# A spectral-gate and gMLP kernel on one core: the TensorE order written by hand, with second-branch matmuls placed into the transform's waits

## The chip, the cores and the metric

The kernel runs on one core of one Trainium2 chip. The metric is the device time of one execution in microseconds (us). Profiles show the core's span, from its first to its last instruction, which is 1.7 to 2.0 us shorter than the time of the same run. PE is the matrix engine (TensorE), PEld its weight load, DVE is VectorE, ACT is ScalarE, POOL is GpSimd, SP the sync engine, whose queue issues most of the DMAs. PE's results go to PSUM buffers, from which ACT or DVE copies them to SBUF, the on-chip memory: that copy is called the eviction. rstd is one over the square root of variance plus epsilon, bn_stats the DVE instruction that gathers mean and variance (BATCH_NORM_STATS2 in the views), and a slab is a block of 512 rows of `w_sp`, loaded transposed in four pieces.

## The reference

```python
# x, B_x: (1, 2048, 576) bf16     w_in: (576, 4608)     w_sp: (2048, 2048)     w_out: (2304, 576)
xn = layernorm(A_x)
s  = irfft2(rfft2(xn) * (w_r + 1j * w_i))            # branch A: a 2-D Fourier filter
z  = gelu(xn @ w_in)                                 # branch B: gMLP
z1, z2 = z[..., :2304], layernorm(z[..., 2304:])
g  = w_sp @ z2 + b_sp[:, None]
y  = (z1 * g) @ w_out
out = A_x + s * silu(y)
```

(In the reference, branch B is called with the normalised `xn`.)

## The kernel before

Branch A is a chain of matrix products against Fourier tables, and between its stages the data changes layout by going through DRAM:

- `p0`: row block of `xn` times the table of the short axis, evicted and written to DRAM `Ad`.
- `p1`: first half of the long axis; reads `Ad` with another stride, writes `Bd`.
- `p2` and `p3`: second half, multiplied with the filter by DVE in between, and the inverse; reads `Bd`, writes `Ed`.
- `p4`: reads `Ed`, leaves `V` in SBUF. `p5`: `V` to the result `Yd`.

Each of the three passes through DRAM is a wait: the last block must be evicted, written, and read again before the next stage starts. Branch B has much independent work: `z2` (96 units of five 384-column matmuls and one gelu; statistics by DVE on even row blocks, by ACT on odd ones), and then the main loop of 72 steps, each a `z1` tile (5 matmuls) and a `main` tile (16 matmuls), with the output product after each 18 steps.

As program text (cuts are marked):

```python
def ln1(ms):                      # statistics, then normalise, transpose on PE, evict to xnT
    ...
    nc.scalar.activation(out=rs[:], in_=mv[:, :, 1], func=ACT.Sqrt, bias=eps[:], scale=1.0)
    nc.vector.reciprocal(out=rs[:], in_=rs[:])
    for i, m in enumerate(ms):
        ...                       # normalise (DVE), 5 transposes (PE), evict (ACT)

def p0(m):
    ...                           # 10 matmuls
    sg = STG[m % 3]...            # three staging slots
    nc.scalar.activation(out=sg, in_=pa[:, :, 0:L], func=ACT.Identity)
    nc.sync.dma_start(out=Adw[m], in_=sg)

def p23(ch):
    for i in range(0, 8, 2):
        pa = psa.tile(...)        # psa: two buffers, used by p0..p5 and the output
        ...                       # p2: 2 matmuls
        for c in range(2):
            nc.vector.tensor_tensor(out=tt[:, c, :, :], in0=pa..., in1=wt..., op=ALU.mult)
        pb = psa.tile(...)
        ...                       # p3: 4 matmuls on tt, ACT evicts, Ed is written every second pair

with tc.manual_schedule(engines={SP}):       # only the sync queue is in program order
    for ms in ([0], [1], [2, 3], [4, 5, 6, 7], [8, 9, 10, 11], [12, 13, 14, 15]):
        ln1(ms)
        for m in ms: p0(m)
    ...                           # p1_read, load_w, p1, p23_read, p23
    ...                           # constants G4, bias, CESO, first z1 weights
    load_slab(0)                  # four DMA transposes of w_sp
    p4_read(0); p4_read(1)
    for ch in range(4): p4(ch); ...
    for m in range(MT): z2(m)     # 96 units
    z1(0)
    for k in range(NK):
        if q == 0 and 2 * fi < MT: p5(2 * fi); p5(2 * fi + 1)
        ...
        if k + 1 < NK: z1(k + 1)
        main(k)
        ...
```

All engines but SP are ordered by the framework's scheduler at build time. It already moves `z2` matmuls forward into waits of branch A. Once built, the order of a queue is fixed: in experiment 5 PE stands 14.3 us in front of late operands with `z2` work behind them.

Of the kernel before, what the change touches and what calls it, by code (L numbers as in the profile page):

```python
# [11 lines left out]
ACT = mybir.ActivationFunctionType  # L12
# [68 lines left out]
def kernel(  # L81
# [114 lines left out]
    for c in range(1, 4):  # L196
        XC.append(load_x(c))
# [15 lines left out]
    def ln1(ms):  # L213
# [7 lines left out]
        rs = small.tile([P, n], F32, tag=f"rs{n}", bufs=3)  # L221
        nc.scalar.activation(out=rs[:], in_=mv[:, :, 1], func=ACT.Sqrt, bias=eps[:], scale=1.0)
        nc.vector.reciprocal(out=rs[:], in_=rs[:])
        for i, m in enumerate(ms):
            xn = XN[m % 3]
            nc.vector.tensor_scalar(out=xn[:, 0:D], in0=XC[m // 4][:, m % 4, :], scalar1=mv[:, i, 0:1],  # L226
                                    scalar2=rs[:, i:i + 1], op0=ALU.subtract, op1=ALU.mult)
            pt = psh.tile([P, KS, P], BF16, tag="h")
            for ks in range(KS):
                nc.tensor.transpose(pt[:, ks, :], xn[:, ks * P:(ks + 1) * P], ident[:])  # L230
            nc.scalar.activation(out=xnT[:, m, :, :], in_=pt[:], func=ACT.Identity)
# [3 lines left out]
    def p0(m):  # L235
# [5 lines left out]
        sg = STG[m % 3].rearrange("p (c l) -> p c l", c=2)  # L241
        nc.scalar.activation(out=sg, in_=pa[:, :, 0:L], func=ACT.Identity)
        nc.sync.dma_start(out=Adw[m], in_=sg)
# [7 lines left out]
    def p1(ch):  # L251
        ain = AIN[ch]
        av = ain.rearrange("p (s l) -> p s l", s=8)
        bs = BES[ch % 2]
        bv = bs.rearrange("p (s l) -> p s l", s=8)
        for i in range(0, 8, 2):
            pa = psa.tile([P, 2, 512], F32, tag="a")
            for j in range(2):
                nc.tensor.matmul(pa[:, j, 0:L], lhsT=G1[:, ch * 8 + i + j, :], rhs=av[:, i + j, :], start=True, stop=True)
            nc.scalar.activation(out=bv[:, i:i + 2, :], in_=pa[:, :, 0:L], func=ACT.Identity)  # L260
        nc.sync.dma_start(out=rowv(Bd)[:, ch * 8 * L:(ch + 1) * 8 * L], in_=bs)
# [8 lines left out]
    def p23_read(ch):  # L270
        nc.sync.dma_start(out=AIN[ch].rearrange("p (h l) -> p h l", h=8), in_=colv(Bd)[:, ch * 8:(ch + 1) * 8, :])

    def p23(ch):
        ain = AIN[ch].rearrange("p (h l) -> p h l", h=8)
        for i in range(0, 8, 2):
            hh = ch * 8 + i
            wt = WCH[(hh // 4) % 2]
            tt = TT[(i // 2) % 2]
            pa = psa.tile([P, 2, 512], F32, tag="a")
            for j in range(2):  # L280
                nc.tensor.matmul(pa[:, j, 0:L], lhsT=MM[:, 0, :], rhs=ain[:, i + j, :], start=True, stop=True)  # L281
            for c in range(2):
                nc.vector.tensor_tensor(out=tt[:, c, :, :], in0=pa[:, :, 0:L], in1=wt[:, c, hh % 4:hh % 4 + 2, :], op=ALU.mult)  # L283
            pb = psa.tile([P, 2, 512], F32, tag="a")
            for j in range(2):
                for c in range(2):
                    nc.tensor.matmul(pb[:, j, 0:L], lhsT=MM[:, 1 + c, :], rhs=tt[:, c, j, :], start=(c == 0), stop=(c == 1))  # L287
            es = BES[ch % 2].rearrange("p (h l) -> p h l", h=8)
            nc.scalar.activation(out=es[:, i:i + 2, :], in_=pb[:, :, 0:L], func=ACT.Identity)
            if i % 4 == 2:  # L290
                if hh // 4 + 2 < 8:
                    load_w(hh // 4 + 2)
                nc.sync.dma_start(out=colv(Ed)[:, hh - 2:hh + 2, :], in_=es[:, i - 2:i + 2, :])
# [208 lines left out]
```

## Time and profile before

| what | value | view |
|---|---|---|
| time, median of 4 runs | 580.79 us (579.43 to 582.55) | times |
| span of the profiled run (a fifth run, of 578.61 us) | 576.8 us | page |
| sum of all matmuls at their issue pace | about 533 us | order of time, summed |
| first `z1` (start of the main loop) | 161.4 us | order of time, PE |
| PE idle by name before that | 26 us | waits, PE |

The page's first part gives engine, busy time, share of the span and instructions. In its second part one digit stands for 1/40 of the span (14.4 us), in tenths; PEclk is the TensorE clock that was granted.

```profile
PE 545.3 (95%) x3128; PEld 301.3 (52%) x3128; DVE 208.6 (36%) x413; ACT 172.5 (30%) x342; POOL 21.8 (4%) x77
...
PE   4798988999699999999999999999999999999996
...
PEclk9898999999799999999999999999999999999999
```

PE is the only engine that is busy throughout. But for the tail, all that is missing lies in the first 11 digits, 160 us. From the groups of instructions by line (busy, mean ns of one, idle before and its releaser) this is the largest matmul group:

```profile
L388 PE MATMUL pg<-AR,z 128*128 128x512 bf16 x1152 | 260.6, 379 | 0.0
```

379 ns is how long one takes, not how often one starts: matmuls overlap. In the order of time, the first of 16 of L388 starts 3.45 us before the group that follows, so one starts every 216 ns. The sum of such paces is the floor, about 533 us, to which 7 us of start and 5 us of tail are added.

The waits of PE (engine, line, for whom: us in total, times, longest):

```profile
PE pt L230 <- DVE AR L226: 12.0, 4, 6.9
PE pa L304 <- DMA AR<-Ed: 4.3, 1, 4.3
PE pb L287 <- DVE AR L283: 4.2, 5, 1.2
PE pa L259 <- DMA AR<-Ad: 2.1, 1, 2.1
PE ph L341 <- ACT z L347: 2.0, 2, 1.2
```

They are spread: the start, the `Ad` read, the multiplies in p2/p3 (L283), the `Ed` read. The largest single DMA wait has its origin in the sync queue. In order of time (start, us, engine, line, operation, count), the sync queue issues:

```profile
131.96 13.77 SPq L370 DMA_TRANSPOSE AR<-in_B_w_sp_dram  x4
145.77 1.06 SPq L296 DMA_DIRECT2D AR<-Ed  x2
```

Four transposes of the slab take 13.77 us to issue, and the `Ed` read stands behind them. This is one pass through p2/p3 on PE, with the idle time before a group in brackets:

```profile
87.28 0.41 PE L281 MATMUL pa<-AR 128*128 128x289 bf16 x2
87.53 1.30 PE L341 MATMUL ph<-RW,xnT 128*128 128x384 bf16 x7
90.03 0.30 PE L287 MATMUL pb<-AR 128*128 128x289 bf16 x1 [1.20 <-DVE AR L283]
```

`p2` (L281), then the `z2` matmuls that the scheduler put into the wait, then `p3` (L287), still 1.2 us too early for the multiplies.

### The profile page before, as it was taken

How to read it: one execution, taken by the hardware profiler on the slowest of the kernel's cores; microseconds unless marked ns; L12 is line 12 of the kernel's file. 1: busy time of each engine (PE TensorE's matmuls, PEld its weight loads, DVE VectorE, ACT ScalarE, POOL GpSimd, SP SyncE). 2: the span in 40 equal slices, each digit the busy share in tenths (PEclk: the TensorE clock that was granted, in tenths of full speed). 3: DMA queues.
4: the chain of work that ended last, by engine and by line, in shares of the span. 5: the costliest groups of instructions: out<-in, count | busy, mean ns of one | idle time of the engine just before them, and what ended most of it. 6: DMA issues, size and time to landing. Idle time of an engine off the chain costs nothing.

```text
span 576.8 us, 7798 instructions
## 1 busy us (share of the span) xinstructions
PE 545.3 (95%) x3128; PEld 301.3 (52%) x3128; DVE 208.6 (36%) x413; ACT 172.5 (30%) x342; POOL 21.8 (4%) x77
## 2 busy tenths in 40 slices
PE   4798988999699999999999999999999999999996
PEld 2575545555455544447544444754444474444464
DVE  6602367864563432223322222332222232222223
ACT  3856976778461211110111111111111111111101
POOL 2000111112010000000000000000000000000000
PEclk9898999999799999999999999999999999999999
DMA  8737485549613249311661111164111122111003
GB/s 300 214 94 248 160 228 164 161 116 254 174 58 92 73 121 251 95 51 32 136 143 32 31 32 51 55 149 108 32 31 32 51 63 73 31 32 53 0 12 92
DMA packets 80965, 59.47 MB, mean 103 GB/s; under 512 B 36768, under 2 KB 75552, under 8 KB 80672
## 3 DMA queue, kind: packets, MB, share of 16 engines
q1 hardware_dynamic: 80928, 58.97, 37.3%
q8 instruction: 24, 0.39, 0.3%
q14 instruction: 13, 0.11, 0.1%
HBM read 38.74 MB, written 11.82 MB: 88 GB/s over the span
## 4 chain that ended last, share of the span: by engine, by line
PE 81%; ACT 5%; DVE 4%; SPq 4%; DMA 3%; issue 2%; POOL 1%; DVEq 0%; ACTq 0%; POOLq 0%
PE pg L388 43%; PE ph L380 13%; PE po L402 12%; PE ph L341 5%; SPq L370 2%; PE pa L239 2%; PE pa L319 2%; ACT TH L350 2%; DMA AR<-in_A_x_dram 1%; DVE st L348 1%; DVE AR L283 1%; PE pa L304 1%; PE pb L287 1%; DMA AR<-Ed 1%; DMA AR<-Ad 1%
## 5 line engine op out<-in xcount | busy, mean ns | idle before, releaser
L388 PE MATMUL pg<-AR,z 128*128 128x512 bf16 x1152 | 260.6, 379 | 0.0
L388 PEld LDWEIGHTS <-z 128*128 128x128 bf16 x1152 | 112.7, 98 | 135.6
L391 DVE TENSOR_TENSOR AR<-pg,AR 128x512 bf16<-128x512 f32 x72 | 49.8, 691 | 230.4 <-PE pg L388 230.4
L382 ACT ACTIVATE AR<-ph 128x512 bf16<-128x512 f32 x72 | 42.9, 597 | 241.7 <-PE ph L380 241.7
L341 PE MATMUL ph<-RW,xnT 128*128 128x384 bf16 x480 | 90.2, 333 | 2.0 <-ACT z L347 2.0
L380 PE MATMUL ph<-xnT,AR 128*128 128x512 bf16 x360 | 89.5, 379 | 0.0
L402 PE MATMUL po<-AR,RW 128*128 128x288 bf16 x576 | 71.2, 286 | 0.0
L341 PEld LDWEIGHTS <-xnT 128*128 128x128 bf16 x480 | 47.7, 100 | 32.4 <-issue 6.4
L402 PEld LDWEIGHTS <-RW 128*128 128x128 bf16 x576 | 56.4, 98 | 14.9
L380 PEld LDWEIGHTS <-AR 128*128 128x128 bf16 x360 | 35.1, 98 | 40.2
L348 DVE BATCH_NORM_STATS2 st<-z 128x6 f32<-128x384 bf16 x48 | 24.1, 548 | 31.4 <-ACT z L347 31.4
L406 ACT ACTIVATE TH<-po 128x576 f32<-128x576 f32 x16 | 10.4, 651 | 77.6 <-PE po L402 77.6
L392 DVE TENSOR_TENSOR RW<-AR 128x512 bf16<-128x512 bf16 x72 | 30.6, 425 | 6.7
L407 DVE SCALAR_TENSOR_TENSOR AR<-TH,po 128x576 bf16<-128x576 f32 x16 | 12.1, 754 | 47.5 <-ACT TH L406 47.5
L345 ACT ACTIVATE z<-ph 128x384 bf16<-128x384 f32 x48 | 23.6, 493 | 10.9 <-PE ph L341 10.6
L283 DVE TENSOR_TENSOR AR<-pa,AR 128x578 bf16<-128x578 f32 x32 | 22.7, 751 | 5.1 <-PE pa L281 5.0
L347 ACT ACTIVATE z<-ph 128x384 bf16<-128x384 f32 x48 | 21.1, 495 | 5.8 <-PE ph L341 5.7
L239 PE MATMUL pa<-AR,xnT 128*128 128x289 bf16 x160 | 22.4, 299 | 0.2
L239 PEld LDWEIGHTS <-xnT 128*128 128x128 bf16 x160 | 16.1, 102 | 5.8 <-issue 0.3
L362 DVE TENSOR_SCALAR z<-z,mv,rs 128x2304 bf16<-128x2304 bf16 x16 | 14.1, 879 | 13.9 <-POOL rs L210 13.9
L230 PE MATMUL pt<-ident,AR 128*128 128x128 bf16 x80 | 7.1, 248 | 12.0 <-DVE AR L226 12.0
L287 PE MATMUL pb<-AR 128*128 128x289 bf16 x64 | 12.9, 288 | 5.0 <-DVE AR L283 4.2
(50 smaller groups left out, 241.0 us busy)
## 6 DMA issues: line engine op xcount, KB each, us to landing
AR<-in_B_w_in_dram SPq DMA_DIRECT2D x24, 384.0 KB, 3.5
AR<-in_A_x_dram SPq DMA_DIRECT2D x20, 144.0 KB, 2.3
AR<-in_B_w_out_dram SPq DMA_DIRECT2D x1, 2592.0 KB, 12.3
Ad<-AR SPq DMA_DIRECT2D x16, 144.5 KB, 2.6
AR<-Ad SPq DMA_DIRECT2D x4, 578.0 KB, 5.6
AR<-in_A_w_r_dram SPq DMA_DIRECT2D x16, 144.5 KB, 2.9
AR<-in_A_w_i_dram SPq DMA_DIRECT2D x16, 144.5 KB, 3.3
Bd<-AR SPq DMA_DIRECT2D x4, 578.0 KB, 3.3
```

The source lines that it names most:

```text
L239: nc.tensor.matmul(pa[:, c, 0:L], lhsT=xnT[:, m, ks, :], rhs=CDSD[:, ks, c, :], start=(ks == 0), stop=(ks == KS - 1))
L283: nc.vector.tensor_tensor(out=tt[:, c, :, :], in0=pa[:, :, 0:L], in1=wt[:, c, hh % 4:hh % 4 + 2, :], op=ALU.mult)
L341: nc.tensor.matmul(ph[:], lhsT=xnT[:, m, ks, :], rhs=WIN2[:, ks, n * ZC:(n + 1) * ZC], start=(ks == 0), stop=(ks == KS - 1))
L345: nc.scalar.activation(out=zc, in_=ph[:], func=ACT.Gelu_apprx_tanh, accum_out=sm[:, n:n + 1])
L347: nc.scalar.activation(out=zc, in_=ph[:], func=ACT.Gelu_apprx_tanh)
L348: nc.vector.bn_stats(out=st[:, n, :], in_=zc)
L380: nc.tensor.matmul(ph[:].rearrange("p (a t) -> p a t", a=4), lhsT=wb[:, ks, (fi % WG) * P:(fi % WG + 1) * P], rhs=xnT[:, 4 * q:4 * q + 4, ...
L382: nc.scalar.activation(out=Z1T[k % 3], in_=ph[:], func=ACT.Gelu_apprx_tanh)
L388: nc.tensor.matmul(pg[:], lhsT=Z2[m][:, fi * P:(fi + 1) * P], rhs=SLAB[q % 2][:, m, :], start=(m == 0), stop=(m == MT - 1))
L391: nc.vector.tensor_tensor(out=tmp, in0=pg[:], in1=BB[:, q * 512:(q + 1) * 512], op=ALU.add)
L392: nc.vector.tensor_tensor(out=U[k % NU], in0=tmp, in1=Z1T[k % 3], op=ALU.mult)
L402: nc.tensor.matmul(po[:, h, 0:H2], lhsT=U[(q * FT + fi) % NU][:, i * P:(i + 1) * P], rhs=WOUT[:, fi, h * H2:(h + 1) * H2], start=(fi == 0) ...
```

## The change

The intent is to keep PE fed during the first 160 us. No matmul is added or removed. The diff, cut to its core:

```diff
+            rs = rstd_of(mv, n, f"l1{n}")      # row groups from 4 on: rstd by POOL pow, not ACT sqrt
...
     def p0(m):
-        sg = STG[m % 3].rearrange("p (c l) -> p c l", c=2)
+        sg = reg("BES", (m % 8) * 2 * L, 2 * L).rearrange("p (c l) -> p c l", c=2)
-        nc.sync.dma_start(out=Adw[m], in_=sg)
+        nc.gpsimd.dma_start(out=Adw[m], in_=sg)
...                                             # p1: evictions alternate ACT, DVE; p23 split into p2, p3
-    with tc.manual_schedule(engines={mybir.EngineType.SP}):
+    with tc.manual_schedule(engines={mybir.EngineType.SP, mybir.EngineType.PE}):
...
+        load_w(0); load_w(1); <load G4>; <load CESO>          # constants early
+        for m in range(MT):
+            ...                                                # ln1 when due
+            if m + 1 < MT:
+                xpose(m + 1)                                   # transposes one block ahead
+            p0(m)
+            if m >= 9:
+                fill(2)                                        # two z2 units
         for ch in range(4):
             p1_read(ch)
+        fill(10)
+        for s2 in range(0, N2, 2):
+            p1(s2)
+            fill(1)
         for ch in range(4):
             p23_read(ch)
+        fill(9)
+        p2(0)
+        for hh in range(0, N2, 2):
+            fill(1)
+            if hh + 2 < N2:
+                p2(hh + 2)                                     # p2 one step ahead
+            fill(1)
+            p3(hh)
+            if hh % 4 == 2 and hh >= 20:
+                load_slab(0, [hh // 4 - 5])                    # three slab pieces here
+        p4_read(0); load_win1(0); load_slab(0, [3]); p4_read(1); load_win1(1); <load bias>
-        <p4, then all z2>
+        fill(MT * NZC)                                         # the last 15 units
         z1(0)
+        au = [partial(p4, u) for u in range(4 * NLC)] + [partial(p5, j) for j in range(MT)]
         for k in range(NK):
+            units = au[3 * k:3 * k + 3]                        # p4 and p5 inside the first ten main steps
+            if units: units[0]()
...
-            main(k)
+            main(k, units[1:])
```

The last two odd row blocks also move their statistics from ACT to DVE, the `Bd` reads fill the input buffers in another order, and the evictions of `p4` change places between ACT and DVE.

More of the change, by code (lines that the diff above doesn't have):

```diff
@@ L1 @@
 from contextlib import ExitStack
-import math
+from functools import partial
 import numpy as np
@@ L195 @@
     nc.sync.dma_start(out=CDSD, in_=cd_cdsd.ap().rearrange("p (k c l) -> p k c l", k=KS, c=2))
-    for c in range(1, 4):
-        XC.append(load_x(c))
+    XC += [load_x(1), load_x(2), load_x(3)]
     nc.gpsimd.memset(WIN2[KT:P, KS - 1, :], 0.0)
@@ L220, in ln1, with xpose @@
             nc.vector.bn_aggr(out=mv[:, i, :], in_=st[:])
-        rs = small.tile([P, n], F32, tag=f"rs{n}", bufs=3)
-        nc.scalar.activation(out=rs[:], in_=mv[:, :, 1], func=ACT.Sqrt, bias=eps[:], scale=1.0)
-        nc.vector.reciprocal(out=rs[:], in_=rs[:])
-        for i, m in enumerate(ms):
-            xn = XN[m % 3]
-            nc.vector.tensor_scalar(out=xn[:, 0:D], in0=XC[m // 4][:, m % 4, :], scalar1=mv[:, i, 0:1],
-                                    scalar2=rs[:, i:i + 1], op0=ALU.subtract, op1=ALU.mult)
-            pt = psh.tile([P, KS, P], BF16, tag="h")
-            for ks in range(KS):
-                nc.tensor.transpose(pt[:, ks, :], xn[:, ks * P:(ks + 1) * P], ident[:])
-            nc.scalar.activation(out=xnT[:, m, :, :], in_=pt[:], func=ACT.Identity)
+        if ms[0] < 4:
+            rs = small.tile([P, n], F32, tag=f"rs{n}", bufs=3)
+            nc.scalar.activation(out=rs[:], in_=mv[:, :, 1], func=ACT.Sqrt, bias=eps[:], scale=1.0)
+            nc.vector.reciprocal(out=rs[:], in_=rs[:])
+        else:
+            rs = rstd_of(mv, n, f"l1{n}")
+        for i, m in enumerate(ms):
+            ln1_of[m] = (mv[:, i, 0:1], rs[:, i:i + 1])
+    ln1_of = {}
+    def xpose(m):
+        xn = XN[m % 3]
+        mean, rs = ln1_of[m]
+        nc.vector.tensor_scalar(out=xn[:, 0:D], in0=XC[m // 4][:, m % 4, :], scalar1=mean, scalar2=rs,
+                                op0=ALU.subtract, op1=ALU.mult)
+        pt = psh.tile([P, KS, P], BF16, tag="h")
+        for ks in range(KS):
+            nc.tensor.transpose(pt[:, ks, :], xn[:, ks * P:(ks + 1) * P], ident[:])
+        nc.scalar.activation(out=xnT[:, m, :, :], in_=pt[:], func=ACT.Identity)
     Adw = Ad[:].rearrange("(c m p) l -> m p c l", c=2, p=P)
@@ L249, in p1_read, with p1 @@
         nc.sync.dma_start(out=AIN[ch], in_=rowv(Ad)[:, ch * 8 * L:(ch + 1) * 8 * L])
-    def p1(ch):
-        ain = AIN[ch]
-        av = ain.rearrange("p (s l) -> p s l", s=8)
-        bs = BES[ch % 2]
-        bv = bs.rearrange("p (s l) -> p s l", s=8)
-        for i in range(0, 8, 2):
-            pa = psa.tile([P, 2, 512], F32, tag="a")
-            for j in range(2):
-                nc.tensor.matmul(pa[:, j, 0:L], lhsT=G1[:, ch * 8 + i + j, :], rhs=av[:, i + j, :], start=True, stop=True)
+    def p1(s2):
+        ch, i = s2 // 8, s2 % 8
+        av = AIN[ch].rearrange("p (s l) -> p s l", s=8)
+        bv = BES[ch % 2].rearrange("p (s l) -> p s l", s=8)
+        pa = psa.tile([P, 2, 512], F32, tag="a")
+        for j in range(2):
+            nc.tensor.matmul(pa[:, j, 0:L], lhsT=G1[:, s2 + j, :], rhs=av[:, i + j, :], start=True, stop=True)
+        if i % 4 == 0:
             nc.scalar.activation(out=bv[:, i:i + 2, :], in_=pa[:, :, 0:L], func=ACT.Identity)
-        nc.sync.dma_start(out=rowv(Bd)[:, ch * 8 * L:(ch + 1) * 8 * L], in_=bs)
+        else:
+            nc.vector.tensor_copy(out=bv[:, i:i + 2, :], in_=pa[:, :, 0:L])
+        if i == 6:
+            nc.sync.dma_start(out=rowv(Bd)[:, ch * 8 * L:(ch + 1) * 8 * L], in_=BES[ch % 2])
     wqv = [w.rearrange("(q h) l -> q h l", h=N2) for w in (A_w_r, A_w_i)]
@@ L270, in p23_read @@
     def p23_read(ch):
-        nc.sync.dma_start(out=AIN[ch].rearrange("p (h l) -> p h l", h=8), in_=colv(Bd)[:, ch * 8:(ch + 1) * 8, :])
-    def p23(ch):
-        ain = AIN[ch].rearrange("p (h l) -> p h l", h=8)
-        for i in range(0, 8, 2):
-            hh = ch * 8 + i
-            wt = WCH[(hh // 4) % 2]
-            tt = TT[(i // 2) % 2]
-            pa = psa.tile([P, 2, 512], F32, tag="a")
-            for j in range(2):
-                nc.tensor.matmul(pa[:, j, 0:L], lhsT=MM[:, 0, :], rhs=ain[:, i + j, :], start=True, stop=True)
-            for c in range(2):
-                nc.vector.tensor_tensor(out=tt[:, c, :, :], in0=pa[:, :, 0:L], in1=wt[:, c, hh % 4:hh % 4 + 2, :], op=ALU.mult)
-            pb = psa.tile([P, 2, 512], F32, tag="a")
-            for j in range(2):
-                for c in range(2):
-                    nc.tensor.matmul(pb[:, j, 0:L], lhsT=MM[:, 1 + c, :], rhs=tt[:, c, j, :], start=(c == 0), stop=(c == 1))
-            es = BES[ch % 2].rearrange("p (h l) -> p h l", h=8)
-            nc.scalar.activation(out=es[:, i:i + 2, :], in_=pb[:, :, 0:L], func=ACT.Identity)
-            if i % 4 == 2:
-                if hh // 4 + 2 < 8:
-                    load_w(hh // 4 + 2)
-                nc.sync.dma_start(out=colv(Ed)[:, hh - 2:hh + 2, :], in_=es[:, i - 2:i + 2, :])
@@ new lines, in p23_read, with p2 @@
+        nc.sync.dma_start(out=AIN[ch ^ 2].rearrange("p (h l) -> p h l", h=8), in_=colv(Bd)[:, ch * 8:(ch + 1) * 8, :])
+    def p2(hh):
+        ain = AIN[(hh // 8) ^ 2].rearrange("p (h l) -> p h l", h=8)
+        wt = WCH[(hh // 4) % 2]
+        tt = TT[(hh // 2) % 2]
+        pa = psa.tile([P, 2, 512], F32, tag="a")
+        for j in range(2):
+            nc.tensor.matmul(pa[:, j, 0:L], lhsT=MM[:, 0, :], rhs=ain[:, hh % 8 + j, :], start=True, stop=True)
+        for c in range(2):
+            nc.vector.tensor_tensor(out=tt[:, c, :, :], in0=pa[:, :, 0:L], in1=wt[:, c, hh % 4:hh % 4 + 2, :], op=ALU.mult)
+        if hh % 4 == 2 and hh // 4 + 2 < 8:
+            load_w(hh // 4 + 2)
@@ new lines, in p3 @@
+    def p3(hh):
+        tt = TT[(hh // 2) % 2]
+        i = hh % 8
+        pb = psa.tile([P, 2, 512], F32, tag="a")
+        for j in range(2):
+            for c in range(2):
+                nc.tensor.matmul(pb[:, j, 0:L], lhsT=MM[:, 1 + c, :], rhs=tt[:, c, j, :], start=(c == 0), stop=(c == 1))
+        es = BES[(hh // 8) % 2].rearrange("p (h l) -> p h l", h=8)
+        nc.scalar.activation(out=es[:, i:i + 2, :], in_=pb[:, :, 0:L], func=ACT.Identity)
+        if i % 4 == 2:
+            nc.sync.dma_start(out=colv(Ed)[:, hh - 2:hh + 2, :], in_=es[:, i - 2:i + 2, :])
@@ L295, in p4_read, with p4 @@
     def p4_read(ch):
         nc.sync.dma_start(out=AIN[ch % 2], in_=rowv(Ed)[:, ch * 8 * L:(ch + 1) * 8 * L])
-    def p4(ch):
-        ain = AIN[ch % 2]
-        av = ain.rearrange("p (s l) -> p s l", s=8)
-        for lc in range(NLC):
-            pa = psa.tile([P, 2, 4, P], F32, tag="a")
-            for i in range(8):
-                nc.tensor.matmul(pa[:, i // 4, i % 4, :], lhsT=av[:, i, LC0[lc]:LC0[lc] + P], rhs=G4[:, ch * 8 + i, :],
-                                 start=True, stop=True)
-            vd = V[:, lc, :, ch * 8:ch * 8 + 8, :].rearrange("p c s t -> p s c t")
-            vs = pa[:].rearrange("p a s (c t) -> p (a s) c t", c=2)
-            if (ch * NLC + lc) % 2 == 0:
-                nc.vector.tensor_copy(out=vd, in_=vs)
-            else:
-                nc.scalar.activation(out=vd, in_=vs, func=ACT.Identity)
+    def p4(u):
+        ch, lc = u // NLC, u % NLC
+        av = AIN[ch % 2].rearrange("p (s l) -> p s l", s=8)
+        pa = psa.tile([P, 2, 4, P], F32, tag="a")
+        for i in range(8):
+            nc.tensor.matmul(pa[:, i // 4, i % 4, :], lhsT=av[:, i, LC0[lc]:LC0[lc] + P], rhs=G4[:, ch * 8 + i, :],
+                             start=True, stop=True)
+        vd = V[:, lc, :, ch * 8:ch * 8 + 8, :].rearrange("p c s t -> p s c t")
+        vs = pa[:].rearrange("p a s (c t) -> p (a s) c t", c=2)
+        if u % 2 == 1:
+            nc.vector.tensor_copy(out=vd, in_=vs)
+        else:
+            nc.scalar.activation(out=vd, in_=vs, func=ACT.Identity)
+        if lc == NLC - 1 and ch < 2:
+            p4_read(ch + 2)
@@ L329, with z2 @@
     junk = TH[:].rearrange("p a d -> p (a d)").bitcast(BF16)
-    def z2(m):
-        on_act = m % 2 == 1
+    z2s = {}
+    def z2(u):
+        m, n = u // NZC, u % NZC
+        on_act = m % 2 == 1 and m < MT - 2
+        if n == 0:
+            z2s["s"] = small.tile([P, NZC + 1], F32, tag="sm2", name="sm2") if on_act else \
+                small.tile([P, NZC, 6], F32, tag="st2", name="st2")
+        st = z2s["s"]
+        ph = psh.tile([P, ZC], F32, tag="h")
+        for ks in range(KS):
+            nc.tensor.matmul(ph[:], lhsT=xnT[:, m, ks, :], rhs=WIN2[:, ks, n * ZC:(n + 1) * ZC],
+                             start=(ks == 0), stop=(ks == KS - 1))
+        zc = Z2[m][:, n * ZC:(n + 1) * ZC]
+        if on_act:
+            nc.scalar.activation(out=zc, in_=ph[:], func=ACT.Gelu_apprx_tanh, accum_out=st[:, n:n + 1])
+        else:
+            nc.scalar.activation(out=zc, in_=ph[:], func=ACT.Gelu_apprx_tanh)
+            nc.vector.bn_stats(out=st[:, n, :], in_=zc)
+        if n < NZC - 1:
+            return
         mv = small.tile([P, 1, 2], F32, tag="mvz")
         if on_act:
-            sm = small.tile([P, NZC + 1], F32, tag="sm2")
-        else:
-            st = small.tile([P, NZC, 6], F32, tag="st2")
-        for n in range(NZC):
-            ph = psh.tile([P, ZC], F32, tag="h")
-            for ks in range(KS):
-                nc.tensor.matmul(ph[:], lhsT=xnT[:, m, ks, :], rhs=WIN2[:, ks, n * ZC:(n + 1) * ZC],
-                                 start=(ks == 0), stop=(ks == KS - 1))
-            zc = Z2[m][:, n * ZC:(n + 1) * ZC]
-            if on_act:
-                nc.scalar.activation(out=zc, in_=ph[:], func=ACT.Gelu_apprx_tanh, accum_out=sm[:, n:n + 1])
-            else:
-                nc.scalar.activation(out=zc, in_=ph[:], func=ACT.Gelu_apprx_tanh)
-                nc.vector.bn_stats(out=st[:, n, :], in_=zc)
-        if on_act:
-            nc.scalar.activation(out=junk, in_=Z2[m][:], func=ACT.Square, accum_out=sm[:, NZC:NZC + 1])
-            nc.vector.reduce_sum(out=mv[:, 0, 0:1], in_=sm[:, 0:NZC], axis=mybir.AxisListType.X)
+            nc.scalar.activation(out=junk, in_=Z2[m][:], func=ACT.Square, accum_out=st[:, NZC:NZC + 1])
+            nc.vector.reduce_sum(out=mv[:, 0, 0:1], in_=st[:, 0:NZC], axis=mybir.AxisListType.X)
             nc.gpsimd.tensor_scalar(out=mv[:, 0, 0:1], in0=mv[:, 0, 0:1], scalar1=1.0 / Fh, scalar2=0.0,
@@ L355, in z2 @@
             nc.gpsimd.tensor_tensor(out=sq[:], in0=mv[:, 0, 0:1], in1=mv[:, 0, 0:1], op=ALU.mult)
-            nc.gpsimd.tensor_scalar(out=mv[:, 0, 1:2], in0=sm[:, NZC:NZC + 1], scalar1=1.0 / Fh, scalar2=0.0,
+            nc.gpsimd.tensor_scalar(out=mv[:, 0, 1:2], in0=st[:, NZC:NZC + 1], scalar1=1.0 / Fh, scalar2=0.0,
                                     op0=ALU.mult, op1=ALU.add)
@@ L365, with load_slab @@
     wspv = B_w_sp.rearrange("t (b p) -> t b p", p=P)
-    def load_slab(q):
-        for i in range(4):
+    def load_slab(q, parts=range(4)):
+        for i in parts:
             t0 = q * 512 + i * P
@@ L382, in z1, with main @@
         nc.scalar.activation(out=Z1T[k % 3], in_=ph[:], func=ACT.Gelu_apprx_tanh)
-    def main(k):
+    def main(k, between=()):
         q, fi = steps[k]
+        between = list(between)
         pg = psh.tile([P, 512], F32, tag="h")
         for m in range(MT):
+            if m % 8 == 0 and between:
+                between.pop(0)()
             nc.tensor.matmul(pg[:], lhsT=Z2[m][:, fi * P:(fi + 1) * P], rhs=SLAB[q % 2][:, m, :],
@@ L418, with fill @@
     NK = len(steps)
-    with tc.manual_schedule(engines={mybir.EngineType.SP}):
-        for ms in ([0], [1], [2, 3], [4, 5, 6, 7], [8, 9, 10, 11], [12, 13, 14, 15]):
-            ln1(ms)
-            for m in ms:
-                p0(m)
-        nc.sync.dma_start(out=MM, in_=cd_mm.ap().rearrange("p (a k) -> p a k", a=3))
+    zq = iter(range(MT * NZC))
+    def fill(n):
+        for u in zq:
+            z2(u)
+            n -= 1
+            if n == 0:
+                break
+    with tc.manual_schedule(engines={mybir.EngineType.SP, mybir.EngineType.PE}):
+        groups = [[0], [1], [2, 3], [4, 5, 6, 7], [8, 9, 10, 11], [12, 13, 14, 15]]
+        nc.sync.dma_start(out=MM, in_=cd_mm.ap().rearrange("p (a k) -> p a k", a=3))
+        load_w(0)
+        load_w(1)
+        nc.sync.dma_start(out=G4, in_=cd_g4.ap().rearrange("p (s k) -> p s k", s=N2))
+        nc.sync.dma_start(out=CESO, in_=cd_ceso.ap().rearrange("p (a c l) -> p a c l", a=NLC, c=2))
+        ready = 0
+        for m in range(MT):
+            while ready < min(m + 2, MT):
+                ln1(groups[0])
+                for mm in groups.pop(0):
+                    ready = mm + 1
+            if m == 0:
+                xpose(0)
+            if m + 1 < MT:
[3 more added lines that the diff above has]
+                fill(2)
@@ L425 @@
         for ch in range(4):
             p1_read(ch)
-        for ch in range(4):
-            if ch < 2:
-                load_w(ch)
-            p1(ch)
+        fill(10)
+        for s2 in range(0, N2, 2):
+            p1(s2)
+            fill(1)
         for ch in range(4):
             p23_read(ch)
-        for ch in range(4):
-            p23(ch)
+        fill(9)
[8 more added lines that the diff above has]
+                load_slab(0, [hh // 4 - 5])
@@ L435 @@
         for i in range(2):
             nc.gpsimd.memset(WIN1[i][KT:P, KS - 1, :], 0.0)
-        nc.sync.dma_start(out=G4, in_=cd_g4.ap().rearrange("p (s k) -> p s k", s=N2))
-        nc.sync.dma_start(out=BB, in_=B_b_sp.rearrange("(a s) -> a s", a=1).to_broadcast((P, S)))
-        nc.sync.dma_start(out=CESO, in_=cd_ceso.ap().rearrange("p (a c l) -> p a c l", a=NLC, c=2))
-        load_win1(0)
-        load_win1(1)
-        load_slab(0)
-        p4_read(0)
-        p4_read(1)
-        for ch in range(4):
-            p4(ch)
-            if ch < 2:
-                p4_read(ch + 2)
@@ L449 @@
-        for m in range(MT):
-            z2(m)
+        p4_read(0)
+        load_win1(0)
+        load_slab(0, [3])
+        p4_read(1)
+        load_win1(1)
+        nc.sync.dma_start(out=BB, in_=B_b_sp.rearrange("(a s) -> a s", a=1).to_broadcast((P, S)))
+        fill(MT * NZC)
         z1(0)
+        au = [partial(p4, u) for u in range(4 * NLC)] + [partial(p5, j) for j in range(MT)]
+        LAST = (len(au) - 1) // 3
         for k in range(NK):
             q, fi = steps[k]
-            if q == 0 and 2 * fi < MT:
-                p5(2 * fi)
-                p5(2 * fi + 1)
-            if q == 0 and 2 * fi == MT:
+            units = au[3 * k:3 * k + 3]
+            if units:
+                units[0]()
+            if k == LAST + 1:
```

## The prediction

> **What bounds the kernel now.** TensorE (PE). The page gives PE 95% busy, but spans overlap; the issue pace counts. In the order of time, 16 L388 matmuls of 512 columns take 3.45 us, 216 ns each. (The Trainium skill, "TensorE: Matmul & The Clock Gate", section "Wait — 56ns, not 53.3ns?", states 215.7 ns once warm; the trace agrees.) Read the same way: 384 columns 163 ns, 289 about 124, 128 about 60. Summed over all matmuls: about 533 us of the 576.8 us span. From the first z1 (161.4 us) on, PE is dense; the tail is 5 us. The loss lies before: 6.9 us to the first transpose, then about 30. The waits view names, for PE: 12.0 us on DVE normalising x (6.9 of it the start), 4.3 on the Ed read, 4.2 on the L283 multiplies, 2.1 on the Ad read, 2.0 on gelu; the rest is slowed clock (0.91 in 20-60 us) and small waits. At 132-146 us the sync queue issues four slab transposes (13.8 us) ahead of the Ed read that p4 needs.
>
> **What the change does.** No matmul is removed. PE order is fixed by hand: transposes one block ahead of p0, z2 units (5 matmuls, 0.81 us, one gelu) in every DMA or evict wait, p2 one step ahead of p3, all p4 and p5 moved into the first ten main steps, so the Ed chain hides behind 15 z2 units. Constants load early, three of four slab transposes move into p23, Ad writes move to the POOL queue with eight staging slots, later rows take rstd from POOL, so gelu needs no wait for the last sqrt.
>
> **Cost by stage (estimates from trace durations).**
> - To the first fill, about 25 us: DVE normalisation (last at 25 before) still bounds.
> - p0 with 14 units, to 46 us; 10 more units cover evict, Ad write, Ad read: p1 starts near 56 us (52 before), 24 units done against 10: gain 7.
> - p1: 16 x 1.06 us; 9 units nearly cover Bd. p2 starts near 82.5 us with 49 units (79.2 and 34 before): gain 9 in all.
> - p2/p3: PE needs 2.4 us a step. DVE needs 1.5 (multiplies) + 1.1 (bn_stats) + normalisation = 2.95 on even rows, 1.85 on odd; ACT on odd rows 0.65 + 1.4 + a third of a 2.3 us Square = 2.8. About 42 us, to 124.5, with 81 units against 64: gain 13.
> - 15 units, 12 us: main begins near 137 us, not 161.
> - main: 414 us (z1 78, pg 249, p4 6, p5 12, po 71), dense as before; tail 5.
>
> Span about 557, a gain of 20; times lie 2 to 5 us above the profile's span: **561 us, 80% range 552 to 571**. Faster by over 2%: 0.80; within 2%: 0.18; slower: 0.02.
>
> **What would show it.** Right: first z1 near 137 us; PE waits on Ed and Ad reads gone, on multiplies not; L388 still 379 ns; DVE over 85% busy in p2/p3. Wrong in a step: p1 later than 58 us (POOL slow); p2/p3 over 45 us; new waits in the first ten main steps on p4/p5 evictions, bias or the last slab piece.
>
> **What would make it wrong.** A fixed PE order cannot slip past a late operand: each late DVE, ACT or POOL result stops everything behind it. POOL carries both rstd and Ad writes, whose issue cost there this trace does not show. Slab transposes may slow the Ed writes. If all goes better than my DVE and ACT sums allow, the floor is about 546 us.

## The result and the profile after

The changed kernel took 562.88 us (median of 10 runs, 561.16 to 564.39), the kernel before 580.41 us in the same rounds (15 runs). The ratio of times is 0.9701, 95% interval 0.9679 to 0.9723. Ratios here are the mean time of one kernel's fast runs over that of the other's of the same rounds, so they are not quite the ratio of the medians quoted. The span fell from 576.8 to 561.1 us.

The page after, parts 1 and 2, and from part 3 the software queue:

```profile
PE 539.9 (96%) x3128; PEld 299.9 (53%) x3128; DVE 217.0 (39%) x424; ACT 166.5 (30%) x323; POOL 37.1 (7%) x95
...
PE   4999989999999999999999999999999999999995
...
PEclk9999998999999999999999999999999999999999
...
q0 software_dynamic: 768, 2.37, 1.3%
```

The matmuls are the same 3128. The first digits have filled up; one clock dip is left, in slice 7. The waits of PE after:

```profile
PE pt L238 <- DVE AR L234: 8.2, 2, 6.9
PE pa L289 <- DMA AR<-Bd: 3.0, 1, 3.0
PE pa L247 <- DMA AR<-c_cdsd: 1.4, 1, 1.4
PE pb L301 <- DVE AR L291: 0.8, 2, 0.4
PE pb L301 <- ACT AR L303: 0.8, 2, 0.4
PE ph L397 <- DMA AR<-in_B_w_in_dram: 0.6, 1, 0.6
PE pa L265 <- DMA AR<-Ad: 0.3, 1, 0.3
```

The wait on `Ed` is gone, that on `Ad` is 0.3 us, and the wait on the multiplies fell from 4.2 to 0.8 us. The wait on `Bd` grew from 0.3 to 3.0 us. In the order of time, PE around it and at the start of the main loop:

```profile
74.17 8.29 PE L355 MATMUL ph<-RW,xnT 128*128 128x384 bf16 x50
85.45 0.64 PE L289 MATMUL pa<-AR 128*128 128x289 bf16 x2 [2.99 <-DMA AR<-Bd]
85.88 1.81 PE L355 MATMUL ph<-RW,xnT 128*128 128x384 bf16 x5
...
128.07 12.56 PE L355 MATMUL ph<-RW,xnT 128*128 128x384 bf16 x75
140.46 1.24 PE L397 MATMUL ph<-xnT,AR 128*128 128x512 bf16 x5
141.54 0.61 PE L315 MATMUL pa<-AR 128*128 128x128 bf16 x8
```

Five matmuls of 384 columns take 1.81 us right after the gap, against 0.97 us elsewhere: the clock was halved for a moment (granted clock 0.50 in 86 to 88 us). That does not follow from the wait alone: p4_first, sqrt_all and ad_sync below have 3.0 to 3.1 us of it at the same place, and a clock of 1.00. Main begins at 140.5 us; `p4` (L315) follows without a wait. From here the two kernels do nearly the same work. The main loop starts 20.9 us earlier, and 80 more of the 96 `p4` matmuls (about 4.5 us at 56 ns) are now still to come: 16.4 us, and the span gained 15.7.

Stage by stage, read from the order of time of PE:

| stage begins | before, us (z2 units done) | after, us (z2 units done) | predicted for after |
|---|---|---|---|
| `p1` | 52.0 (10.4) | 57.0 (24) | 56 (24) |
| `p2` | 79.2 (33.4) | 85.5 (49) | 82.5 (49) |
| last `p3` ends | 124.6 (65.6) | 128.2 (81) | 124.5 (81) |
| first `z1` | 161.4 | 140.5 | 137 |

Why was `Bd` late? The last `p1` matmul starts at 73.9 us. Its eviction is DVE's (L269), and DVE got to it here:

```profile
75.66 0.88 DVE L379 TENSOR_SCALAR z<-z,mv,rs 128x2304 bf16<-128x2304 bf16 x1 [0.52 <-POOL rs L209]
76.45 1.01 DVE L362 BATCH_NORM_STATS2 st<-z 128x6 f32<-128x384 bf16 x2
77.38 0.74 DVE L269 CAST AR<-pa 128x578 bf16<-128x578 f32 x1
```

and DVE's queue had itself been held by ACT, which worked on the sum of squares of the row block before:

```profile
71.95 2.12 ACT L367 ACTIVATE TH<-z 128x2304 bf16<-128x2304 bf16 x1
```

So the eviction ended 3 us after it could have, if DVE had taken it first: a normalisation and two bn_stats, which nobody waits for here, stood ahead of it in DVE's queue. The `Bd` write could have left 2.7 us earlier, for it also needs an eviction by ACT, which ended at 75.5 us behind that same sum of squares. This is read from the trace; no run here reordered those queues. Experiment 12 tests it in part: with each bn_stats 0.2 us shorter, the eviction started 3.1 us after the last `p1` matmul instead of 3.5, and the wait on `Bd` fell from 3.0 to 2.5 us.

### The profile page after: what moved, and what is told of

Its sections match the earlier page's. It is cut to its first block, busy times and chain, and to the rows that moved or that the text cites. A ratio compares the mean times of both kernels' runs of the same rounds, so it can differ in the third digit from the quotient of the medians.

```text
span 561.1 us, 7803 instructions
## 1 busy us (share of the span) xinstructions
PE 539.9 (96%) x3128; PEld 299.9 (53%) x3128; DVE 217.0 (39%) x424; ACT 166.5 (30%) x323; POOL 37.1 (7%) x95
## 4 chain that ended last, share of the span: by engine, by line
PE 86%; DMA 4%; DVE 3%; ACT 2%; SPq 2%; issue 1%; POOL 1%; DVEq 0%; POOLq 0%; ACTq 0%
PE pg L408 42%; PE ph L397 13%; PE po L422 13%; PE ph L355 9%; PE pa L247 3%; PE pa L332 2%; SPq L387 1%; DMA AR<-in_A_x_dram 1%; ACT TH L367 1%; PE pb L301 1%; PE pa L315 1%; DVE st L362 1%; DMA AR<-Bd 1%; PE pa L289 1%; DMA AR<-in_B_w_in_dram 1%
## 5 line engine op out<-in xcount | busy, mean ns | idle before, releaser
L355 PE MATMUL ph<-RW,xnT 128*128 128x384 bf16 x480 | 88.2, 329 | 0.0
L426 ACT ACTIVATE TH<-po 128x576 f32<-128x576 f32 x16 | 10.4, 651 | 77.6 <-PE po L422 77.6
L362 DVE BATCH_NORM_STATS2 st<-z 128x6 f32<-128x384 bf16 x54 | 27.5, 547 | 8.6 <-ACT z L361 8.5
L361 ACT ACTIVATE z<-ph 128x384 bf16<-128x384 f32 x54 | 24.9, 493 | 11.5 <-PE ph L355 11.3
L291 DVE TENSOR_TENSOR AR<-pa,AR 128x578 bf16<-128x578 f32 x32 | 23.0, 744 | 7.2 <-PE pa L289 7.2
L247 PE MATMUL pa<-AR,xnT 128*128 128x289 bf16 x160 | 24.3, 301 | 1.4 <-DMA AR<-c_cdsd 1.4
L367 ACT ACTIVATE TH<-z 128x2304 bf16<-128x2304 bf16 x7 | 14.9, 2122 | 0.2
## 6 DMA issues: line engine op xcount, KB each, us to landing
AR<-in_A_w_r_dram SPq DMA_DIRECT2D x16, 144.5 KB, 3.4
Ad<-AR POOLq DMA_DIRECT2D x16, 144.5 KB, 8.0
AR<-in_A_w_i_dram SPq DMA_DIRECT2D x16, 144.5 KB, 3.0
```

What stands on the lines that cost most here:

```text
L247: nc.tensor.matmul(pa[:, c, 0:L], lhsT=xnT[:, m, ks, :], rhs=CDSD[:, ks, c, :], start=(ks == 0), stop=(ks == KS - 1))
L291: nc.vector.tensor_tensor(out=tt[:, c, :, :], in0=pa[:, :, 0:L], in1=wt[:, c, hh % 4:hh % 4 + 2, :], op=ALU.mult)
L355: nc.tensor.matmul(ph[:], lhsT=xnT[:, m, ks, :], rhs=WIN2[:, ks, n * ZC:(n + 1) * ZC], start=(ks == 0), stop=(ks == KS - 1))
L361: nc.scalar.activation(out=zc, in_=ph[:], func=ACT.Gelu_apprx_tanh)
L362: nc.vector.bn_stats(out=st[:, n, :], in_=zc)
```

## The experiments

The main theory (A): the gain is the sum of several waits before the main loop, each hidden by moving independent matmuls into it; what counts is that the fill is as long as the wait. Rivals: (B) the hand-fixed PE order as such, which the scheduler would spoil; (C) moving `p4` into the main loop is the gain; (D) ACT was swapping its function tables between sqrt and gelu, and rstd on POOL ends that; and that the DMA queue moves did it. Times are medians; the ratio is to the kernel before in the same rounds. Differences from the changed kernel go across rounds, so medians and ratios can differ by some us; where it matters, both are given.

### 1. The fixed order given back: auto_pe

```diff
-    with tc.manual_schedule(engines={mybir.EngineType.SP, mybir.EngineType.PE}):
+    with tc.manual_schedule(engines={mybir.EngineType.SP}):
```

> The changed kernel with the TensorE order given back to the scheduler (only the sync queue stays in hand order); all else is kept. Theory A (the gain comes from the order in which the fill work is written and from what it hides; the fixed order itself is not needed): within 3 us of the changed kernel, first z1 at 139 to 143 us. Theory B (only an order fixed by hand gives the gain, the scheduler would undo it): over 570 us, first z1 later than 147 us, PE waits on the Ad, Bd or Ed reads back.

Measured: 562.77 us, ratio 0.9647 (0.9595 to 0.9698), first `z1` at 140.4 us. The PE waits moved a little between stages (1.5 us on `Bd`, 1.4 on the `z1` weights). Theory B falls: given the new program text, the scheduler builds an order worth the same. What counts is the new program, not who enforces the order of PE.

### 2. p4 ahead of the main loop again: p4_first

```diff
+        for u in range(4 * NLC):
+            p4(u)
         z1(0)
-        au = [partial(p4, u) for u in range(4 * NLC)] + [partial(p5, j) for j in range(MT)]
+        au = [partial(p5, j) for j in range(MT)]
```

> The changed kernel with all twelve p4 units ahead of the first z1 again, p5 alone between main steps. Theory A (several hidden waits share the gain; p4 in main hides only the later Ed reads): 3 to 6 us slower than the changed kernel, with PE waiting on Ed reads for 2 to 5 us between p4 units. Theory C (moving p4 into main is the gain): 12 us or more slower, that is, near the time of before.

Measured: 570.82 us, ratio 0.9802 (0.9764 to 0.9840): about 8 us slower than the changed kernel by the medians and 6 by the ratios, at or above what I expected and less than theory C asks. The reason is also not the one I gave. The waits of PE at `p4` (L315):

```profile
PE pa L315 <- DVE AR L320: 3.7, 3, 2.6
...
PE pa L315 <- DMA AR<-Ed: 0.6, 2, 0.4
```

`p4` back to back waits for its own evictions (1.0 us on ACT or 1.2 on DVE for a unit that takes PE 0.45), with only two PSUM buffers, and DVE was still busy with statistics. The gaps also cost clock: 0.83 in 140 to 160 us. Among main's matmuls the evictions have time.

### 3. p4 in the main loop, alone, on the kernel before: p4_only

The same rewriting of `p4`, `p5` and `main` as in the change, on the kernel before; nothing else.

> The kernel before with one part of the change alone: p4 units and p5 spread over the first ten main steps; everything else, the queue order too, as before. Theory A (this part is worth what its removal cost, 8 us, since it hides the Ed wait of 4.3 us, the stretched p4 evictions and the slowed clock of 140 to 160 us): 5 to 9 us faster than before. Theory C (it is the whole gain): 14 us or more faster. Rival (without the slab pieces moved, the Ed read stays late and p4 in main stalls instead): less than 3 us faster, with PE waits on the Ed read inside the first main steps.

Measured: 573.35 us against 579.50, ratio 0.9879 (0.9837 to 0.9921): 6 us gained, first `z1` at 147.8 us instead of 161.4, one wait of 1.2 us left on `Ed`. As theory A has it: a third to a half of the gain, whichever end one starts from (6 to 7 us alone, 6 to 8 when removed).

### 4. Ed read ahead of the slab transposes, on the kernel before: slab_late

```diff
-        load_slab(0)
         p4_read(0)
         p4_read(1)
+        load_slab(0)
```

> The kernel before with one swap on the sync queue: the first two Ed reads are issued ahead of the four slab transposes. Theory A (the 13.8 us of transpose issue held the Ed read back, so p4 waited 4.3 us): the PE wait on Ed is gone and the kernel is 3 to 6 us faster, first z1 at 155 to 158 us. Rival (the transposes then come late for the first pg, or the p4 evictions bound that stage): within 2 us of before, with a new PE wait on the slab or slow p4 units.

Measured: 577.80 us, ratio 0.9948 (0.9906 to 0.9991): 1.7 us faster by the medians, 3 by the ratio (0.5 to 5.5), so the time alone does not tell the two theories apart. The trace does: the first `z1` is at 162.7 us, not at 155 to 158, and the wait on `Ed` is not gone. The first `Ed` read came early, but PE then waited for a later one, 1.8 and 3.4 us:

```profile
PE pa L304 <- DMA AR<-Ed: 5.1, 2, 3.4
```
The third and fourth reads need the buffers of the first two, and now stand behind the transposes. The jam was moved, not removed. This swap of the queue order alone is not the gain.

### 5. p2 no longer one step ahead: no_ahead

```diff
-        p2(0)
         for hh in range(0, N2, 2):
             fill(1)
-            if hh + 2 < N2:
-                p2(hh + 2)
+            p2(hh)
             fill(1)
             p3(hh)
```

> The changed kernel with p2 no longer one step ahead: one fill unit, p2, one fill unit, p3 of the same step. DVE needs 1.5 us for the two multiplies, one unit covers 0.81. Theory A (running p2 one step ahead is what brings p2/p3 to 2.46 us a step): a PE wait on the DVE multiplies of 0.7 to 1 us in most of the 16 steps, p2/p3 longer by 8 to 14 us, the kernel 8 to 14 us slower. Rival (DVE and ACT load set the pace of p2/p3, not the order): within 3 us of the changed kernel.

Measured: 581.15 us, ratio 1.0025 (0.9981 to 1.0068). The whole gain is gone. p2/p3 took 61 us instead of 43. The waits of PE:

```profile
PE pb L301 <- DVE AR L291: 14.3, 20, 2.2
```

One step of it, in order of time:

```profile
94.85 0.97 PE L355 MATMUL ph<-RW,xnT 128*128 128x384 bf16 x5
95.87 0.30 PE L301 MATMUL pb<-AR 128*128 128x289 bf16 x1
96.99 0.53 PE L301 MATMUL pb<-AR 128*128 128x289 bf16 x3 [0.82 <-DVE AR L291]
```

The fill between `p2` and `p3` is 0.8 us, the two multiplies take 1.5, and a fixed order stops there each time. The direction was as expected, the size above it (18 us, not 8 to 14).

### 6. The same, ordered by the scheduler: no_ahead_auto

The diff of no_ahead and that of auto_pe together.

> The kernel without p2 one step ahead (18 us slower than the changed one), but with the TensorE order given to the scheduler. Theory A (a fixed order with too little fill between p2 and p3 stops the engine; the scheduler moves ready z2 work into the wait, as in the kernel before, where p2/p3 took 45 us): p2/p3 back to 43 to 48 us, kernel within 5 us of the changed kernel. Rival (the p2-then-p3 order itself is slow, whoever places the fill): over 575 us.

Measured: 568.68 us, ratio 0.9801 (0.9766 to 0.9836), p2/p3 45.7 us. PE in order of time:

```profile
91.79 0.30 PE L301 MATMUL pb<-AR 128*128 128x289 bf16 x1
91.93 0.65 PE L355 MATMUL ph<-RW,xnT 128*128 128x384 bf16 x3
92.46 0.53 PE L301 MATMUL pb<-AR 128*128 128x289 bf16 x3
```

The scheduler put three `z2` matmuls between the first `p3` matmul, which needs one multiply, and the others, which need the second. So it rescues 12 of the 18 us. What is left against the changed kernel is 6 us, a little over the 5 that I allowed (against auto_pe, its true pair, 6 by the medians and 9 by the ratios): the look-ahead is worth 6 to 9 us to a scheduled order and 18 to a fixed one. Little of the 6 is lost inside p2/p3, whose 45.7 us hold 35 `z2` units where the changed kernel's 42.8 hold 32. The scheduler takes these units from the stretch before the main loop, and PE waits there instead: 1.2 us on `Ed`, 2.5 on the `z1` weights, with a clock of 0.91 in 140 to 160 us.

### 7. Ad writes back on the sync queue: ad_sync

```diff
-        nc.gpsimd.dma_start(out=Adw[m], in_=sg)
+        nc.sync.dma_start(out=Adw[m], in_=sg)
```

> The changed kernel with the sixteen Ad writes back on the sync queue, in program order, so behind the early constant loads, which keep that queue busy until 31 us. Theory A (the POOL queue is needed because the constants were moved up in the sync queue): the first Ad write goes out after 30 us instead of 17, its staging slot holds p0 of row block 8 back, a PE wait of 4 to 9 us at 20 to 35 us, kernel 3 to 9 us slower than the changed one. Rival (the waits are covered, the queue of the Ad writes does not matter, or HBM writes of 2.6 us instead of 8 us make up for it): within 2 us.

Measured: 573.22 us, ratio 0.9902 (0.9859 to 0.9944): 10 us slower than the changed kernel by the medians and 12 by the ratios, more than the 3 to 9 that I expected. The sync queue and the wait it makes (the second fence is the waits view):

```profile
29.01 30.19 SPq L251 DMA_DIRECT2D Ad<-AR  x16
```

```profile
PE pa L247 <- ACT AR L250: 8.0, 1, 8.0
```

The first `Ad` write leaves at 29.0 us, behind the constants. p0's eviction then has no staging slot, and PE stands for 8.0 us; the clock is 0.80 in 20 to 40 us. So the POOL queue is what makes the early constants affordable. Whether either would gain anything on the kernel before was not run. In the changed kernel the writes show as follows (tile view: durations min/median/max, first and last start):

```profile
L251 POOL DMA_DIRECT2D Ad<-AR x16: 723/726/1099, 16.6 to 50.0; - x16
```

The Trainium skill, "DMA: Bandwidth & Descriptors", section "SWDGE vs HWDGE vs iDMA", says that a DMA issued from GpSimd has its descriptors computed in software there, and the setup on the sync queue is faster. As far as the time to issue goes, the trace agrees: 0.73 us of POOL for one write against 0.36 us on the sync queue (tile view of this run). The landing times do not separate the two paths: 2.6 to 9.8 us from POOL in the changed kernel, 2.2 to 9.6 us from SP in this run.

### 8. sqrt on ACT for all rows: sqrt_all

```diff
-        if ms[0] < 4:
-            <ACT sqrt, DVE reciprocal>
-        else:
-            rs = rstd_of(mv, n, f"l1{n}")
+        <ACT sqrt, DVE reciprocal>
```

> The changed kernel with the square root on ScalarE plus reciprocal for all row groups, as before. Theory A (the last sqrt still runs before the first gelu at 29 us, so nothing needed the POOL path; it only adds about 1.3 us of latency at 15 us): two table loads as now, the PE wait of 1.3 us at 17 us gone, the span 0 to 1.5 us shorter. Theory D (sqrt and gelu mix and tables are swapped): four or more table loads of 1.28 us and p1 starting 3 us later or more.

Measured: 563.42 us, ratio 0.9676 (0.9638 to 0.9714): no difference that can be told from the changed kernel. Two table loads of 1.28 us in both, as the Trainium skill states for one load ("ScalarE: Activation LUTs", section "What ACT_TABLE_LOAD costs": about 1283 ns). Theory D falls, and so does the small gain that I expected: PE's waits for the normalisation stayed, 8.7 us in two waits against 8.2. The POOL path is neutral here.

### 9. Four more units ahead of p2: fill13

```diff
-        fill(9)
+        fill(13)
         p2(0)
```

> The changed kernel with 13 instead of 9 fill units ahead of p2, so 11 instead of 15 ahead of main. Theory A (the 3.0 us PE wait on the Bd read and the slowed clock after it are a gap that four units of 0.81 us fill): no PE wait on Bd, granted clock 1.0 in 80 to 100 us, main 1 to 4 us earlier, unless the slab piece or the first weights of z1 then come late, which would show as PE waits before the first pg. Rival: the gap only moves to the end of p2/p3, where the Ed chain is then covered by 3.3 us less: same time within 1 us with a new PE wait of 2 to 3 us on Ed, the slab or the z1 weights.

Measured: 566.99 us (564.96 to 572.50), ratio 0.9752 (0.9689 to 0.9816): slower by 4 us by the medians and 3 by the ratios, with intervals that just overlap. The wait on `Bd` is gone, as expected, but the first `p3` then waited 2.1 us on the multiplies, and the first `z1` 3.8 us on its weights, whose DMA is issued only after the `Ed` writes. (The profile is of the slowest of its runs, so its sizes are high.) The gap went to other places, and grew.

### 10 and 11. Two attempts to mend that: early_fill13 and combo

early_fill13 adds to fill13: `load_win1(0)` at step 26 of p2/p3, slab pieces at steps 18, 22, 26 and 30. combo has the slab pieces at steps 16, 20, 24 and 28 instead, loads the bias first, and starts `p4` one main step later:

```diff
-            units = au[3 * k:3 * k + 3]
+            units = au[3 * k - 3:3 * k] if k > 0 else []
```

> The changed kernel with 13 fill units ahead of p2 (11 ahead of main), the first weights of z1 loaded in p2/p3 at step 26 instead of after it, and all four slab pieces issued in p2/p3, from step 18 on. Theory A (fill13 alone lost because z1 then waited 3.8 us on its weights and the clock fell; the Bd gap itself was filled): no PE wait on Bd and none over 1 us on the z1 weights, first z1 at 136 to 139 us, 2 to 4 us faster than the changed kernel, that is 559 to 561 us. Rival (11 units do not cover the Ed chain, whatever the queue order): PE waits of 2 us or more before the first pg, no faster than the changed kernel.

> An attempt at a better kernel: 13 fill units ahead of p2; slab pieces at steps 16, 20, 24 and 28 of p2/p3, so not right ahead of an Ed write; first z1 weights at step 26; bias loaded right after p2/p3; p4 starts one main step later, so that its Ed read has 6 us more. Theory A (the gaps left are single waits, and what was lost in the two earlier tries was the Ed chain and the z1 weights behind slab pieces): first z1 at 136 to 139 us, no PE wait over 1 us from there on, 1 to 4 us faster than the changed kernel (559 to 562 us). Rival (p2/p3 and its DVE and ACT load set main's start; a unit taken from one gap is missed in another): 562 to 565 us, new waits on the multiplies in p2/p3.

Measured: early_fill13 564.47 us, ratio 0.9727 (0.9686 to 0.9767), with 1.8 us of PE wait on `Ed` before the first `p4`; no faster, as the rival said. combo 561.26 us, ratio 0.9677 (0.9648 to 0.9707). Its interval overlaps that of the changed kernel (0.9679 to 0.9723), so it isn't shown to be faster, and it isn't slower. The two largest waits of PE in combo after that at the start:

```profile
PE pb L301 <- DVE AR L291: 2.9, 3, 2.1
PE pg L408 <- DVE z L379: 1.2, 1, 1.2
```

The first of these is again a late DVE, in order of time:

```profile
85.09 0.88 DVE L379 TENSOR_SCALAR z<-z,mv,rs 128x2304 bf16<-128x2304 bf16 x1 [0.52 <-POOL rs L209]
85.88 1.93 DVE L362 BATCH_NORM_STATS2 st<-z 128x6 f32<-128x384 bf16 x4
87.73 1.41 DVE L291 TENSOR_TENSOR AR<-pa,AR 128x578 bf16<-128x578 f32 x2
```

The multiplies (L291), for which PE waits, stand behind a normalisation and four statistics. Both theories were half right: the waits on `Ed`, the slab and the weights can be moved away, and a wait on DVE takes their place.

### 12. Less DVE work in p2/p3: half_bn

```diff
-            nc.vector.bn_stats(out=st[:, n, :], in_=zc)
+            nc.vector.bn_stats(out=st[:, n, :], in_=zc[:, 0:ZC // 2])   # wrong statistic, on purpose
```

> The changed kernel with bn_stats over only the first 192 of each 384 columns of z2; a wrong statistic on purpose, to take DVE work out of p2/p3. Theory A (on rows whose statistics DVE takes, DVE at about 2.95 us a step sets the pace against 2.46 us elsewhere): the steps of 2.9 to 3.0 us shrink to about 2.5, PE waits on the multiplies gone, p2/p3 1 to 2 us shorter, kernel 0.5 to 2 us faster. Rival (the late normalisation behind the Square on ScalarE makes those steps long): step times unchanged.

Measured: 561.35 us, ratio 0.9676 (0.9644 to 0.9709), so not shown to be faster than the changed kernel; bn_stats 350 ns instead of 547. The start times of `p3` in the changed kernel show its slow steps on one pair of row blocks:

```profile
101.27 0.66 PE L301 MATMUL pb<-AR 128*128 128x289 bf16 x4
104.21 0.66 PE L301 MATMUL pb<-AR 128*128 128x289 bf16 x4 [0.40 <-ACT AR L303]
107.25 0.66 PE L301 MATMUL pb<-AR 128*128 128x289 bf16 x4 [0.43 <-DVE AR L291]
```

Steps of 2.94 and 3.04 us, where the next takes 2.46. With half the statistics the same steps are:

```profile
99.26 0.66 PE L301 MATMUL pb<-AR 128*128 128x289 bf16 x4
102.20 0.66 PE L301 MATMUL pb<-AR 128*128 128x289 bf16 x4 [0.40 <-ACT AR L303]
104.84 0.66 PE L301 MATMUL pb<-AR 128*128 128x289 bf16 x4
```

2.94 and 2.64 us. The step that waited for DVE shrank by 0.4 us, and the one that waits for ACT did not. There are two such pairs in p2/p3, and a new wait of 0.8 us on DVE appeared elsewhere in it. p2/p3 took 41.4 us instead of 42.8. In this run the clock also did not fall after the `Bd` wait of 2.5 us, which accounts for about 1.1 us of that (the first two units took 0.97 us each, not 1.81 and 1.24). So DVE load as such is worth less than 1 us there. Theory A holds for single steps and not as the bound of the stage.

## Why the prediction was right or wrong

Right overall: 562.88 us measured, 561 predicted, inside the range, and faster by 3.0%, where over 2% was forecast. That the number came so close is partly luck: the span missed by 4.1 us (561.1 against about 557), and the prediction added 4 us from span to time, where these runs show 1.8.

- "From the first z1 on, PE is dense; the tail is 5 us." Right. L388 stayed at 379 ns, and the gain in main's start, less the moved `p4`, is the gain in span within 1 us.
- "p1 starts near 56 us, 24 units done." Measured 57.0 with 24. Right within 1 us; POOL was not slow enough to matter, since the ten units covered the chain (wait 0.3 us).
- "9 units nearly cover Bd; p2 starts near 82.5 us." Wrong by 3.0 us, in three parts of about 1 us each: `p1` began at 57.0 instead of 56; its 16 steps, each with a unit, took 17.9 us instead of 17.0 (16 x 1.06); and behind the nine units PE stood 3.0 us, where the sum leaves 2.2 (56 + 17.0 + 9 x 0.81 = 80.3, against 82.5). The cost that it nowhere names is the eviction that stands in DVE's queue behind statistics: from the start of the last `p1` to `p2` it was 8.9 us before and 11.5 after. Had the `Bd` write left the 2.7 us earlier that the trace allows, the nine units would nearly have covered `Bd` (an estimate: 0.3 us of wait left). The shift reaches the first `z1` (140.5 instead of 137) and is most of the 4.1 us by which the span missed.
- "p2/p3: about 42 us", held by DVE (2.95 us on even rows) and ACT (2.8 on odd ones). The sum was right, 42.8 us; the reasons only in part. 15 steps took 2.57 us on average; only four of them were near 2.95, odd rows ran at 2.46, and the way to the first `p3` was slow because the clock fell after the `Bd` gap (3.6 us from the first `p2` to the first `p3`, 2.1 in half_bn, where it did not fall). DVE was 84% busy from 87 to 128 us, just under the 85% that I named. What brings the stage there is the look-ahead (no_ahead), which my sum took for granted.
- "PE waits on Ed and Ad reads gone, on multiplies not." Right, though the latter are only 0.8 us.
- "A fixed PE order cannot slip past a late operand." Right: no_ahead against no_ahead_auto shows it with 12 us. In the changed kernel it does no harm (auto_pe).

Where the gain comes from. Two ways to count it in the two traces agree on its size. By stage, with a `z2` unit at 0.81 us, the table gives 6.0 us up to the start of `p1` (13.6 more units done, 5.0 us later), 0.4 from there to `p2`, 2.4 in p2/p3, and 7.6 from there to the first `z1`, with the 4.5 us of moved `p4` taken off: 16.4 in all. (The prediction's gains to these points, 7, 9, 13 and 20, came out as 6.0, 6.4, 8.8 and 16.4; for the end of p2/p3 it had also counted 64 units before, where the trace has 65.6.) By cause, the named waits of PE fell from 25.9 to 15.1 us in all, and before the change the granted clock was 0.91 in 20 to 40 us, 0.91 in 40 to 60 and 0.83 in 140 to 160, where after it only 80 to 100 us has 0.91. That is 10.8 us of waiting and some 5 us of slow clock (an estimate: the missing shares of these 20 us, 7.0 less 1.8). So about a third of the gain is clock. That the shorter waits bring it is likely but not shown, since waits of 3 us did not always cost clock.

By the runs, `p4` in the main loop is worth 6 to 8 us and the look-ahead 6 to 9 under a scheduled order, most of that in later waits. What is then left, up to 5 us, is a difference and was not measured alone, nor is it certain that such parts add up; the 6 us before `p1` (the fill and the earlier transposes) have no run of their own. POOL rstd brought nothing, the `Ad` writes on POOL undo a jam that the early constants make. What stays open: whether an eviction placed ahead of the statistics in DVE's queue would recover the 2.7 us at `Bd`; half_bn recovered 0.5 of it, and no run tried the order.

## What to carry to other kernels

A wait is hidden when the work put into it is as long as the whole chain it covers, and that chain includes the queue of the engine that evicts, not only the DMA: look at what stands ahead of the last eviction before counting fill units. When a fixed order is used on PE, put each producer far enough ahead of its consumer that the engine in between can finish, for a fixed order turns each shortfall into a stop. Spread small matmul groups with slow evictions among large ones rather than running them back to back, and when one gap is filled, look where its units are now missing.

## What the Trainium skill lacked or had wrong

- "TensorE: Matmul & The Clock Gate", section "HAM oscillation — how this bites in real kernels", has as its abstract rule no PE-idle gaps over about 3.4 us. Here shorter gaps were followed by matmuls at half pace: 3.0 us in the changed kernel and 2.1 us in combo (1.81 us for five matmuls that take 0.97), while 2.5 us in half_bn, and 3.0 to 3.1 us in p4_first, sqrt_all and ad_sync, cost no clock. Gaps under the rule can cost clock, and not every time; what decides it is not shown here.
- "DMA: Bandwidth & Descriptors", section "Anatomy of one DMA — SWDGE (gpsimd) path", gives about 2.0 us plus bytes / 436e3 for one DMA from GpSimd, which would be 2.3 us for 144.5 KB (an estimate from that fit). Here those writes, beside constant loads, took 2.6 to 9.8 us to land. The page's figure is the lower end; from the sync queue they took as long (2.2 to 9.6 us) under the same load.
- "DMA: Bandwidth & Descriptors", section "Latency and other measured facts", gives 261 GB/s as the effective bandwidth of a DMA transpose whose middle dimension is not contiguous, and 350 to 400 where it is. Neither that section nor the one on DMA transposes says how long a large transpose holds the queue that issues it: here the issue of four pieces of 512 KB took 13.77 us in the kernel before (about 150 GB/s, worked out from these two numbers), with all later transfers of that queue behind them.
